# A two-branch kernel on one core: every instruction recorded and issued in the order of a list schedule

## The chip, the cores and the metric

The kernel runs on one core of a Trainium2 chip. The metric is the device time of one execution in microseconds (us), the median of the runs shown. Engines are named as the profile names them: PE (matmul), PEld (its weight loads), DVE (vector), ACT (scalar), POOL, SP. SP and ACT issue transfers from their own instruction streams, and POOL issues some too.

## The reference

Two independent branches are computed on 2048 tokens by 640 channels and concatenated.

Branch A, per channel: a 4-tap shift of `k`, a product with `v`, a causal convolution of length 2048 with the kernel `ssm_k` (by way of a transform), a skip term, a product with `q`:

```
k_shift = sum_t k_pad[:, t:t+S] * shift_k[:, 3-t];   kv = k_shift * v
y = irfft(rfft(kv) * rfft(ssm_k))[:S] + kv * ssm_D;   out_A = q * y
```

Branch B: attention with 32 heads of 20 channels. The 2048 tokens are cut into 4 segments of 512. In each segment there is causal softmax attention, and a memory of the earlier segments:

```
p = softmax(q k^T * scale + mask);  a_dot = p v
a_mem = (phi(q) M) / (phi(q) z + 1e-6)          # phi(t) = t + 1 if t > 0 else exp(t)
o = g * a_mem + (1 - g) * a_dot;   M += phi(k)^T v;  z += sum phi(k)
out_B = concat(o) @ wo
```

## The kernel before, in words

Branch A runs in 5 blocks `dp` of 128 channels. A block loads `sk`, `kr` (transposed by the transfer), `vt` and `qd`; PE does the shift (`pks`, L202) and a forward transform of the kernel and of the product (`pf`, L218), which ACT copies out into `F` (L221); DVE does the butterflies (L229 to L238), the pointwise products (`S`, L251 to L256) and the butterflies back (L261 to L272); PE transforms back (`py`, L283), DVE multiplies by `qd` (`outa`, L284) and POOL stores it (L285).

Branch B runs in 8 units `u`: segment `u // 2`, half `u % 2` of the heads. A unit's projection has four pieces of 128 tokens: 15 matmuls (`kqv`, L312), three copies by ACT (L314), and two transposing transfers on SP that make `KT` (L317) and `QT` (L318). The step `bound` follows: DVE takes a maximum over `KT` (`kam`, L328), PE multiplies (`pb`, L340), ACT copies the result (`bT`, L342) and SP moves it into rows of `QT` by four transfers (L345). POOL spreads `KT` into `KZ` (L377). Then come four groups `g` of four heads: PE makes scores in the banks `stp` (L395), ACT takes their exponential into `ET` (L399, 12 instructions a group, 384 in all), DVE masks (L402), PE multiplies with the values into the one bank `po` (L412, L415), DVE takes a reciprocal (`rr`, L418), multiplies by it (`o2`, L425, or L422 in the first segment) and adds the two parts (L426). After the second half of a segment SP transposes the result (`oT`, L432), PE projects it (`pfo`, L441), ACT copies it out (`outb`, L442) and POOL stores it (L443).

PSUM has eight banks in four pools: three for `stp`, two for A, two for `kqv`, `pb`, `pm` and `pfo`, one for `po`.

The order is set in two steps. The program at L496 to L519 merges lists of pieces by hand-given costs, and the framework's own scheduler then orders the single instructions of the pieces on each engine. Each engine works through its stream in order, an instruction at a time; SP's and POOL's transfers do too, and a transfer that waits holds those behind it.

Of the kernel before, what the change touches and what calls it, by code (L numbers as in the profile page):

```python
# [24 lines left out]
KPAD = 16  # L25
# [34 lines left out]

class K3:
    def __init__(self, ctx, tc, A_q, A_k, A_v, A_shift_k, A_ssm_k, A_ssm_D, B_x, B_wq, B_wk, B_wv, B_wo, B_beta, out):
        self.tc = tc
        nc = self.nc = tc.nc
# [6 lines left out]
        self.a_io2 = E(tc.tile_pool(name="a_io2", bufs=1))  # L71
        self.a_work = E(tc.tile_pool(name="a_work", bufs=1))
        self.a_tmp = E(tc.tile_pool(name="a_tmp", bufs=1))
        self.tmp4 = E(tc.tile_pool(name="tmp4", bufs=1))
        self.b_seg = E(tc.tile_pool(name="b_seg", bufs=1))
        self.b_g = E(tc.tile_pool(name="b_g", bufs=2))
        self.b_small = E(tc.tile_pool(name="b_small", bufs=1))
        self.ps_st = E(tc.tile_pool(name="ps_st", bufs=NST, space=PSUM))
        self.ps_a = E(tc.tile_pool(name="ps_a", bufs=NA, space=PSUM))
        self.ps_b = E(tc.tile_pool(name="ps_b", bufs=NB, space=PSUM))  # L80
        self.ps_o = E(tc.tile_pool(name="ps_o", bufs=NO, space=PSUM))
# [6 lines left out]
        def const(name, arr, dt, eng=nc.gpsimd):  # L88
            t = c.tile(list(arr.shape), dt, name=name)
            eng.dma_start(out=t[:], in_=nc.inline_tensor(arr, name="c_" + name).ap())  # L90
            return t
# [6 lines left out]
        def wload(engs, half):  # L98
# [5 lines left out]
            "Wf": lambda: nc.scalar.dma_start(out=self.Wf[:], in_=nc.inline_tensor(Wf_np, name="c_wf").ap()),  # L104
            "Wi": lambda: nc.sync.dma_start(out=self.Wi[:], in_=nc.inline_tensor(Wi_np, name="c_wi").ap()),
# [50 lines left out]
    def bank(self, pool, name):  # L156
        return pool.tile([128, 512], f32, name=name, tag="bank")

    def a_chunks(self, dp):
# [5 lines left out]
        io, wk = self.a_io2, self.a_work  # L165

        def load_sk():
            sk = io.tile([128, S], bf16, name="sk", tag="kT", bufs=2)
            nc.sync.dma_start(out=sk[:], in_=self.ssm_k[dsl, :])
            skp = io.tile([128, 4, 4, 128], bf16, name="skp", tag="kT", bufs=2)  # L170
            nc.vector.tensor_copy(out=skp[:], in_=sk[:].rearrange("d (b p c) -> d c b p", b=4, c=4))
            Drow = st["Drow"] = io.tile([1, 128], bf16, name="Drow", tag="Drow")
            nc.gpsimd.dma_start(out=Drow[:], in_=self.ssm_D[None, dsl])
            kT = st["kT"] = io.tile([128, 4, 4, 128], bf16, name="kT", tag="kT", bufs=2)
            nc.sync.dma_start_transpose(out=kT[:].rearrange("p c b d -> p (c b) d"), in_=skp[:].rearrange("d c b p -> d (c b p)"))

        def load_kv():
            vt = st["vt"] = io.tile([128, 4, 4, 128], bf16, name="vt", tag="vt")
            for b in range(4):
                (nc.scalar if dp == 0 else nc.sync).dma_start(out=vt[:, b], in_=self.v[512 * b:512 * b + 512, dsl].rearrange("(p c) d -> p c d", c=4))  # L180
            kr = st["kr"] = io.tile([128, 4, KPAD + 512], bf16, name="kr", tag="kr")
# [3 lines left out]
            skd = st["skd"] = io.tile([128, 4, 128], bf16, name="skd", tag="skd")  # L185
# [3 lines left out]
        def load_q():  # L189
            qd = st["qd"] = io.tile([128, 4, 4, 128], bf16, name="qd", tag="qd")  # L190
# [3 lines left out]
        def kshift(b):  # L194
            def f():
                kr, vt = st["kr"], st["vt"]
                ps = self.bank(self.ps_a, "pks")
# [8 lines left out]
        def fwd(kind, c):  # L206
            def f():
                if c == 0:
                    st["F"] = wk.tile([128, 4, 2, 512], bf16, name="F", tag="F")
                F = st["F"]  # L210
                for i in range(2):
                    pf = self.bank(self.ps_a, "pf")
# [28 lines left out]
        def pointwise(b):  # L241
            def f():
                Xv = st["X"][:].rearrange("p (i q) (j a d) -> p i (q j) a d", i=2, j=2, a=2)
                Kv = st["K"][:].rearrange("p (t q) (j b d) -> p t (q j) b d", t=2, j=2, b=2)
                if b == 0:
                    st["S"] = wk.tile([128, 2, 2, 8, 2, 128], bf16, name="S", tag="S")
                Sh = st["S"]
                for i in range(2):
# [3 lines left out]
                    else:  # L252
                        shp = [128, 2, 8, 128]
                        pr = self.a_tmp.tile(shp, bf16, name="pr", tag="pr")
# [19 lines left out]
        def inverse(c):  # L274
            def f():
                U, qd = st["U"], st["qd"]
                outa = self.a_tmp.tile([128, 4, 128], bf16, name="outa", tag="outa", bufs=2)
                py = self.bank(self.ps_a, "py")
# [14 lines left out]
    def b_proj_chunks(self, u):  # L293
# [5 lines left out]
        def load():  # L299
            xT = self.b_seg.tile([128, 5, L], bf16, name="xT", tag="xT")  # L300
# [3 lines left out]
        def proj(tci):  # L304
            def f():
# [3 lines left out]
                for i in range(3):  # L309
                    kq = self.bank(self.ps_b, "kqv")  # L310
# [4 lines left out]
                if tci == 0:  # L315
                    self.KTs[u] = self.b_seg.tile([128, 4, L], bf16, name="KT", tag="KT")
                nc.sync.dma_start_transpose(out=self.KTs[u][:, :, tok], in_=KQ[:, 0, :, :])  # L317
                nc.sync.dma_start_transpose(out=QT[:, :, tok], in_=KQ[:, 1, :, :])  # L318
                if s < NS - 1:
                    xm = self.b_small.tile([128, 2, 16, DH], bf16, name="xm", tag="xm")  # L320
# [5 lines left out]
        def bound():  # L326
            kam = self.b_small.tile([128, 4], f32, name="kam", tag="kam")
            V.tensor_reduce(out=kam[:], in_=self.KTs[u][:], axis=AX.X, op=ALU.max, apply_absolute_value=True)  # L328
            A = self.b_small.tile([128, 4, 16], bf16, name="A", tag="A")
            V.tensor_tensor(out=A[:], in0=self.sel[:], in1=kam[:, :, None].to_broadcast([128, 4, 16]), op=ALU.mult)  # L330
            if s > 0:
                nc.scalar.activation(out=PqT[:], in_=QT[:], func=ACTF.Exp)  # L332
                tq = self.tmp4.tile([128, 4, L], bf16, name="tq", tag="tq")
                V.tensor_scalar(out=tq[:], in0=QT[:], scalar1=1.0, scalar2=1.0, op0=ALU.add, op1=ALU.max)
                V.tensor_tensor(out=PqT[:], in0=PqT[:], in1=tq[:], op=ALU.min)
            qabs = self.tmp4.tile([128, 4, L], bf16, name="qabs", tag="tq")
            V.tensor_scalar(out=qabs[:].bitcast(i16), in0=QT[:].bitcast(i16), scalar1=0x7fff, scalar2=None, op0=ALU.bitwise_and)
# [114 lines left out]
def merge(*lists):  # L452
# [97 lines left out]
```

## Time and profile before

| | |
|---|---|
| median of 3 runs | 390.89 us (390.85 to 393.99) |
| the profiled execution | 391.97 us, span 390.0 us |
| mean granted PE clock | 0.949 |
| first exponential (L399) starts | 62.60 us |
| first exponential of the last unit starts | 341.61 us |
| last exponential ends | 365.73 us |

The span is the time from the first to the last instruction of the profiled execution; its own time is 1.97 us longer. The profile's busy time counts a matmul from its start to its modelled end, so matmuls that follow each other overlap. For the table by stage the span is cut where the first exponential starts, where the last unit's attention starts and where its last exponential ends.

### The profile page before, as it was taken

Reading aid. Unit: us, or ns where it says so; the run is one execution under the profiler, and the core shown is the slowest. Engines: PE = TensorE matmul, PEld = TensorE weight load, DVE = VectorE, ACT = ScalarE, POOL = GpSimd, SP = SyncE. Lnnn points to the kernel's source line nnn. Section 1 sums busy time; section 2 is a strip of 40 time slices with the busy share of each in tenths; the row PEclk is TensorE's granted clock in tenths of the full one; section 3 lists DMA queues with packets and bytes.
Section 4 is the critical chain, followed back from the end, with each engine's and each line's share of the span. In section 5 each row is a group of like instructions: output and inputs, shape, how many; then the busy total and the mean of one; then the engine's idle time right before and its main releaser. Section 6 shows DMA issues by size and latency. Waiting matters only on the chain.

```text
span 390.0 us, 8955 instructions
## 1 busy us (share of the span) xinstructions
PE 326.1 (84%) x3466; PEld 222.3 (57%) x3466; DVE 302.2 (77%) x539; ACT 279.6 (72%) x633; POOL 80.1 (21%) x127
## 2 busy tenths in 40 slices
PE   0499288999989879899979898899989898986854
PEld 0377255565756657467656665577756565644543
DVE  1536299999679969994979999989998938989940
ACT  0067127989898858987777888977789788997402
POOL 8400140202042101231131102132022003410032
PEclk9999869999999989899998999899999999999588
DMA  7999874842246674703863365416620533230052
GB/s 202 272 330 184 171 118 100 141 106 46 58 86 144 107 112 88 150 22 80 180 87 76 59 131 113 94 39 133 116 46 18 100 72 75 57 95 2 0 99 91
DMA packets 110266, 40.96 MB, mean 105 GB/s; under 512 B 102624, under 2 KB 107264, under 8 KB 109968
## 3 DMA queue, kind: packets, MB, share of 16 engines
q1 hardware_dynamic: 100768, 29.50, 39.1%
q0 software_dynamic: 5088, 8.09, 8.0%
q10 hardware_dynamic: 4368, 2.81, 2.5%
q8 instruction: 27, 0.44, 0.5%
q14 instruction: 15, 0.12, 0.1%
HBM read 13.36 MB, written 5.24 MB: 48 GB/s over the span
## 4 chain that ended last, share of the span: by engine, by line
PE 44%; ACT 23%; issue 14%; DMA 9%; DVE 5%; SPq 3%; POOL 2%; POOLq 0%; DVEq 0%; ACTq 0%
ACT ET L399 16%; PE kqv L312 13%; PE stp L395 7%; PE po L412 5%; PE pf L218 5%; PE pfo L441 4%; ACT F L221 3%; PE pks L202 3%; DMA QT<-KQ 3%; DMA xT<-in_B_x_dram 2%; DMA KT<-KQ 2%; PE py L283 2%; PE pb L340 2%; SPq L184 2%; ACT PqT L332 1%
## 5 line engine op out<-in xcount | busy, mean ns | idle before, releaser
L399 ACT ACTIVATE ET<-stp 128x512 bf16<-128x512 f32 (+1 forms) x384 | 172.3, 560 | 15.8 <-PE stp L395 12.6
L395 PE MATMUL stp<-QT,KZ 128*128 128x512 bf16 (+3 forms) x512 | 116.3, 306 | 15.5 <-ACT ET L399 11.4
L312 PE MATMUL kqv<-wqkv,xT 128*128 128x320 bf16 x480 | 82.9, 305 | 1.2 <-DMA xT<-in_B_x_dram 0.9
L395 PEld LDWEIGHTS <-KZ 128*128 128x128 bf16 x512 | 48.2, 99 | 51.0 <-issue 36.0
L377 POOL DMA_DIRECT2D KZ<-KT x64 | 39.8, 624 | 131.2 <-PE stp L395 62.0
L312 PEld LDWEIGHTS <-xT 128*128 128x128 bf16 x480 | 45.7, 99 | 21.3 <-issue 2.9
L221 ACT CAST F<-pf 128x512 bf16<-128x512 f32 x80 | 46.2, 628 | 7.1 <-PE pf L218 5.6
L412 PEld LDWEIGHTS <-ET 128*128 128x128 bf16 x1280 | 42.1, 97 | 14.5 <-DVE o L425 5.3
L402 DVE TENSOR_TENSOR ET<-ET,cmask 128x1024 bf16<-128x1024 bf16 x64 | 41.7, 683 | 9.9 <-ACT ET L399 9.9
L412 PE MATMUL po<-Va,ET 128*128 128x21 bf16 x1280 | 44.3, 174 | 2.8 <-DVE o L425 2.2
L202 PE MATMUL pks<-skd,kr 128*128 128x128 bf16 x320 | 28.0, 241 | 17.4 <-DMA kr<-in_A_k_dram 13.1
L314 ACT CAST KQ<-kqv 128x320 bf16<-128x320 f32 x64 | 27.9, 455 | 19.3 <-PE kqv L312 17.6
L218 PEld LDWEIGHTS <-Wf 128*128 128x128 bf16 x320 | 30.5, 99 | 17.6 <-issue 9.3
L202 PEld LDWEIGHTS <-kr 128*128 128x128 bf16 x320 | 23.6, 109 | 21.3 <-DMA kr<-in_A_k_dram 13.3
L441 PE MATMUL pfo<-wo,oT 128*128 128x320 bf16 x160 | 28.8, 314 | 5.8 <-DMA oT<-o_s 5.3
L285 POOL DMA_DIRECT2D out_dram<-outa x20 | 15.7, 784 | 84.3 <-DVE outa L284 66.8
L442 ACT CAST outb<-pfo 128x320 bf16<-128x320 f32 x32 | 13.3, 451 | 23.4 <-PE pfo L441 20.3
L218 PE MATMUL pf<-kT,Wf 128*128 128x256 bf16 x160 | 26.3, 279 | 4.1 <-ACT F L221 2.7
L418 DVE RECIPROCAL rr<-po 128x16 f32<-128x16 f32 (+1 forms) x64 | 15.5, 243 | 14.4 <-PE po L415 10.9
L283 PE MATMUL py<-S,Wi 128*128 128x256 bf16 x160 | 24.9, 287 | 2.0 <-DVE outa L284 2.0
L218 PE MATMUL pf<-vt,Wf 128*128 128x256 bf16 x160 | 24.5, 279 | 2.2 <-ACT F L221 1.5
L441 PEld LDWEIGHTS <-oT 128*128 128x128 bf16 x160 | 15.6, 101 | 13.6 <-DMA oT<-o_s 6.1
(77 smaller groups left out, 418.0 us busy)
## 6 DMA issues: line engine op xcount, KB each, us to landing
KZ<-KT POOLq DMA_DIRECT2D x64, 42.0 KB, 2.3
sk<-in_A_ssm_k_dram SPq DMA_DIRECT2D x5, 512.0 KB
qd<-in_A_q_dram SPq DMA_DIRECT2D x20, 128.0 KB
out_dram<-outa POOLq DMA_DIRECT2D x20, 128.0 KB, 3.2
out_dram<-outb POOLq DMA_DIRECT2D x16, 160.0 KB, 2.2
vt<-in_A_v_dram SPq DMA_DIRECT2D x16, 128.0 KB
Wf<-c_wf ACTq DMA_DIRECT2D x1, 1024.0 KB
Wi<-c_wi SPq DMA_DIRECT2D x1, 1024.0 KB
```

What stands on the lines that cost most here:

```text
L202: nc.tensor.matmul(ps[:, 128 * c:128 * c + 128], lhsT=kr[:, cc, p0:p0 + 128], rhs=st["skd"][:, t, :], start=(t == 0), stop=(t == 3))
L218: nc.tensor.matmul(o, lhsT=Wf[:, h, c, 256 * i + 128 * j:256 * i + 128 * j + 128], rhs=rhs, start=(h == 0), stop=(h == 1 and not last))
L221: nc.scalar.copy(out=F[:, c, i, :], in_=pf[:])
L283: nc.tensor.matmul(pyv[:, :, h, :], lhsT=Wi[:, k, c, 128 * h:128 * h + 128], rhs=U[:, 4 * i + c, 256 * j:256 * j + 256], start=(k == 0), s ...
L312: nc.tensor.matmul(kq[:, 0:320], lhsT=xT[:, cc, tok], rhs=self.wqkv[:, cc, half, i, :], start=(cc == 0), stop=(cc == 4))
L314: nc.scalar.copy(out=dst, in_=kq[:, 0:320].rearrange("p (h d) -> p h d", d=DH))
L377: nc.gpsimd.dma_start(out=self.KZ[gg][rows, :, hl, :], in_=self.KTs[u][rows, 2 * gg:2 * gg + 2, :])
L395: nc.tensor.matmul(sts[j][:, c0:c0 + n], lhsT=KZ[:, g % 2, hl, 128 * kc:128 * kc + 128], rhs=QT[:, g, 128 * kc:L], start=True, stop=True)
L399: nc.scalar.activation(out=ET[:, 2 * hp + j, e0:e0 + width], in_=sts[j][:, 0:width], func=ACTF.Exp, scale=SCALE)
L402: V.tensor_tensor(out=blk, in0=blk, in1=self.cmask[:, None, None, :].to_broadcast([128, 4, 2, 128]), op=ALU.mult)
L412: nc.tensor.matmul(ops[:, qc % 2, hl, 0:DH + 1], lhsT=ET[:, hl, c0:c0 + 128], rhs=Va[:, kc, 4 * g + hl, 0:DH + 1], start=(kc == 0), stop=( ...
L441: nc.tensor.matmul(pf[:, 0:320], lhsT=oT[:, cc, 128 * tci:128 * tci + 128], rhs=self.wo[:, cc, 320 * i:320 * i + 320], start=(cc == 0), st ...
```

## The change: what it does

No instruction is added or taken away: each engine has as many of each operation after as before (3466 matmuls, 539 on DVE, 633 on ACT, 109 transfers on POOL, 189 on SP, 9 on ACT). The order of all of them is new.

While the kernel's functions run, a recorder stands in place of the engines. It keeps each call, joins the matmuls that follow each other in a bank into one unit, and finds by the regions read and written which units depend on which. Each unit gets a price in ns (on ACT for example its elements per partition over 1.152 plus 33), and a list schedule is made: at every moment an engine that is free takes the ready unit of the highest priority. Priorities come from the length of the way to the end, from a table `BIAS` by stage, and from a pass over the program backwards; six passes are made and the shortest is kept. Transfers of inputs are held back until a time that a pass gives. The schedule also gives out the PSUM banks: a unit that opens a bank is taken only when one of its kind is free. The instructions are then issued in that order, and the framework adds the waits but no order of its own.

Besides, all SBUF tiles are now fixed tiles that are used in turn (`ring`) instead of tiles from pools, the butterfly's temporary `T` lies in the odd planes of its own result instead of in a shared tile, and the score matmuls of a pair of heads are issued bank by bank.

```diff
+    def add(self, eng, method, args, kw):
...
+        if method == "matmul" and bank.last is not None and bank.last.eng == "PE":
+            op = bank.last
...
+    def price(self, op, method, out, ins):
...
+        elif op.eng == "ACT":
+            op.dur, op.lat = n / 1.152 + 33, 210.0
...
+    def forward(self, prio, held):
...
+            for e in free:
+                pe, av = pending[e], avail[e]
+                while pe and pe[0][0] <= t:
+                    i = heapq.heappop(pe)[1]
+                    heapq.heappush(av, (prio[i], i))
+                if free[e] > t:
+                    continue
...
+                    if o.new and (not any(x[0] <= t for x in empty[o.bank.kind]) or (o.bank.row and o.bank.seq != row[o.bank.row])):
+                        put_back.append((p, i))
+                        continue
+                    pick = o
+                    break
...
+                if o.dma is not None:
+                    dma_free = max(dma_free, max(t + 1150, end - 50)) + o.dma
+                    fin = dma_free + 450
+                    near = fin
+                else:
+                    fin, near = end + o.lat, end + (0 if e != "PE" else o.lat)
...
+    def emit(self):
+        for o in self.order:
+            for eng, method, args, kw in o.calls:
...
-                T = self.tmp4.tile([128, 2, 2, 512], bf16, name="T", tag="tq")
-                V.tensor_tensor(out=T[:], in0=F[:, 0:2], in1=F[:, 2:4], op=ALU.add)
+                T = X[:, 1:8:2, :].rearrange("p (c i) r -> p c i r", c=2)
+                V.tensor_tensor(out=T, in0=F[:, 0:2], in1=F[:, 2:4], op=ALU.add)
...
-                        for (kc, c0) in spec:
-                            n = L - 128 * kc
-                            for j in range(2):
-                                hl = 2 * hp + j
+                        for j in range(2):
+                            hl = 2 * hp + j
+                            for (kc, c0) in spec:
+                                n = L - 128 * kc
...
+BANKS = {"st": 3, "a": 2, "b": 2, "o": 1}
+BIAS = {
+    ('A', 0, 0): 5055, ('A', 0, 1): 3361, ('A', 0, 10): 288761, ('A', 0, 11): 15357, ('A', 0, 12): 174774, ('A', 0, 13): 17992, ('A', 0, 14): -17162,
...
-    seq += merge(b_main, a_main)
-    for ch, _ in seq:
-        ch()
+    rec.finish()
+    rec.plan(BIAS, HOLD, PASSES, SLACK)
+    with tc.manual_schedule():
+        rec.emit()
```

Three places show how the order moved. In the changed kernel every instruction has the line of the call in `emit`, L435; its tiles carry the names of the rings. The first place is SP's queue at the start, round the last `KT` transfer of unit 0 (the fourth from `KQ`) and the four transfers of `bT`. Before:

```order
L318 DMA_TRANSPOSE QT_114<-KQ_110 128x4x128
L184 DMA_TRANSPOSE kr<-in_A_k_dram 128x512
L192 DMA qd<-in_A_q_dram 128x4x128 x2
L317 DMA_TRANSPOSE KT<-KQ_109 128x4x128
L318 DMA_TRANSPOSE QT_114<-KQ_109 128x4x128
L192 DMA qd<-in_A_q_dram 128x4x128 x2
L169 DMA sk<-in_A_ssm_k_dram 128x2048
L317 DMA_TRANSPOSE KT<-KQ_110 128x4x128
L318 DMA_TRANSPOSE QT_114<-KQ_110 128x4x128
L180 DMA vt<-in_A_v_dram 128x4x128 x4
L175 DMA_TRANSPOSE kT<-skp 128x16x128
L345 DMA QT_114<-bT 1x4x512 x4
```

Now:

```order
L435 DMA_TRANSPOSE KT_114<-KQ_80 128x4x128
L435 DMA_TRANSPOSE QT_85<-KQ_80 128x4x128
L435 DMA wqkv<-in_B_wq_dram 128x5x320
L435 DMA_TRANSPOSE KT_114<-KQ_81 128x4x128
L435 DMA_TRANSPOSE kr_105<-in_A_k_dram 128x512
L435 DMA_TRANSPOSE QT_85<-KQ_81 128x4x128
L435 DMA_TRANSPOSE kr_105<-in_A_k_dram 128x512 x2
L435 DMA vt_104<-in_A_v_dram 128x4x128
L435 DMA_TRANSPOSE kr_105<-in_A_k_dram 128x512
L435 DMA vt_104<-in_A_v_dram 128x4x128
L435 DMA wqkv<-in_B_wv_dram 128x5x320
L435 DMA vt_104<-in_A_v_dram 128x4x128
```

The second block's `kr` loads, the first block's `qd` loads, one weight load, `Wi` and `wo` stood ahead of the last `KT` transfer and stand behind it now; three of the four `bT` transfers follow the last row shown.

The second place is DVE in the last unit, where the `po` bank is read (`rr`, then the product by `rr`). Before:

```order
L418 RECIPROCAL rr<-po 128x16
L267 TENSOR_TENSOR S<-S 128x2048
L425 TENSOR_TENSOR o_5879<-po,rr 128x320
L269 TENSOR_TENSOR S<-S 128x2x512
L426 TENSOR_TENSOR o_s<-o_5879 128x2x80
```

Now:

```order
L435 RECIPROCAL rr_124<-o_68 128x16
L435 TENSOR_TENSOR o_129<-o_68,rr_124 128x320
L435 TENSOR_TENSOR o_s_120<-o_129 128x2x80
L435 TENSOR_TENSOR S_109<-S_109 128x2048
L435 TENSOR_TENSOR ET_122<-ET_122,cmask 128x4x2x128
```

Of the 64 pairs of a reciprocal and its product, 8 stood next to each other before and 60 do now. Instructions that directly follow the one whose result they read went from 58 to 126 of 539 on DVE.

The third place is ACT where unit 6 begins, between its `bT` copy and its first exponential. Before:

```order
L342 CAST bT<-pb 16x512
L399 ACTIVATE ET<-stp 128x512 x3
L399 ACTIVATE ET<-stp 128x256 x2
L221 CAST F<-pf 128x512
L399 ACTIVATE ET<-stp 128x512 x4
L399 ACTIVATE ET<-stp 128x256 x2
L221 CAST F<-pf 128x512
```

Now:

```order
L435 CAST bT_119<-b_66 16x512
L435 CAST F_102<-a_64 128x512
L435 CAST KQ_80<-b_67 128x16x20
L435 CAST KQ_80<-b_66 128x16x20
L435 CAST Va_84<-b_67 128x16x20
L435 CAST KQ_81<-b_66 128x16x20
L435 CAST KQ_81<-b_67 128x16x20
L435 CAST F_102<-a_65 128x512
L435 CAST Va_84<-b_66 128x16x20
L435 ACTIVATE ET_121<-st_61 128x512
```

Exponentials of unit 5 followed the copy before (11 of them); none is left now, and eight copies stand in between. At the other six beginnings of a unit there were 23, 16, 1, 12, 8 and 18 exponentials left before and there are 26, 15, 11, 4, 14 and 11 now (units 1 to 5, and 7).

## Rows read from the trace of the kernel before

**Rows 1.** The page's first section: busy us (share of the span) xinstructions.

```profile
PE 326.1 (84%) x3466; PEld 222.3 (57%) x3466; DVE 302.2 (77%) x539; ACT 279.6 (72%) x633; POOL 80.1 (21%) x127
```

**Rows 2.** Busy time by stage: length, each engine, clock, transfer share, GB/s.

```profile
0.00:40.00 40.00, 24.47 (x190) 18.38 (x191) 15.85 (x28) 15.42 (x35) 13.64 (x21) 1.00 1.02 244
40.00:62.60 22.60, 14.16 (x126) 10.04 (x126) 15.54 (x20) 3.99 (x10) 5.52 (x9) 0.77 0.73 137
62.60:341.60 279.00, 254.12 (x2798) 173.55 (x2797) 239.62 (x436) 235.85 (x534) 54.62 (x88) 0.98 0.45 91
341.60:365.70 24.10, 18.38 (x209) 9.98 (x207) 22.14 (x37) 21.00 (x49) 1.17 (x2) 0.89 0.15 38
365.70:390.00 24.30, 14.93 (x146) 10.39 (x146) 9.01 (x21) 3.34 (x9) 5.19 (x8) 0.78 0.36 76
```

**Rows 3.** The chain of waits at the start: start, length, what.

```profile
43.61 3.56 DMA QT<-KQ
47.37 2.28 DVE kam L328
50.43 1.88 PE pb L340 x4
```

**Rows 4.** SP's queue in order of time: start, length, what it issues.

```profile
25.61 0.60 SPq L107 DMA_DIRECT2D wo<-in_B_wo_dram  x1
26.31 4.11 SPq L184 DMA_TRANSPOSE kr<-in_A_k_dram  x2
31.79 1.25 SPq L184 DMA_TRANSPOSE kr<-in_A_k_dram  x1
34.41 1.25 SPq L184 DMA_TRANSPOSE kr<-in_A_k_dram  x1
35.71 1.34 SPq L192 DMA_DIRECT2D qd<-in_A_q_dram  x2
39.76 1.25 SPq L192 DMA_DIRECT2D qd<-in_A_q_dram  x2
41.79 1.72 SPq L317 DMA_TRANSPOSE KT<-KQ  x1
52.95 3.04 SPq L345 DMA_DIRECT2D QT<-bT  x4
```

**Rows 5.** ACT in order of time at the start; in brackets the idle time before.

```profile
52.34 0.57 ACT L342 CAST bT<-pb 16x512 bf16<-16x512 f32 x1 [11.86 <-PE pb L340]
62.60 1.57 ACT L399 ACTIVATE ET<-stp 128x512 bf16<-128x512 f32 x3 [2.12 <-PE stp L395]
```

**Rows 6.** DVE's waits from 62.6 to 341.6 us: us in total, times, longest.

```profile
DVE ET L402 <- ACT ET L399: 9.9, 8, 5.3
DVE rr L418 <- PE po L415: 8.0, 13, 1.5
DVE kam L328 <- DMA KT<-KQ: 3.7, 2, 2.9
```

**Rows 7.** DVE in order of time in the last unit.

```profile
367.87 0.48 DVE L425 TENSOR_TENSOR o<-po,rr 128x320 bf16<-128x320 f32 x1
368.26 0.68 DVE L272 TENSOR_TENSOR S<-S 128x1024 bf16<-128x1024 bf16 x1
...
373.58 0.49 DVE L425 TENSOR_TENSOR o<-po,rr 128x320 bf16<-128x320 f32 x1
374.11 0.24 DVE L426 TENSOR_TENSOR o_s<-o 128x160 bf16<-128x160 bf16 x1
```

**Rows 8.** The last unit in order of time: ACT, PE and SP.

```profile
341.61 10.53 ACT L399 ACTIVATE ET<-stp 128x512 bf16<-128x512 f32 x24
360.10 4.31 ACT L399 ACTIVATE ET<-stp 128x512 bf16<-128x512 f32 x9 [1.89 <-PE po L415]
365.94 0.49 PE L412 MATMUL po<-Va,ET 128*128 128x21 bf16 x12 [0.97 <-DVE o L425]
373.01 6.44 SPq L432 DMA_TRANSPOSE oT<-o_s  x4
```

More of the change, by code (lines that the diff above doesn't have):

```diff
@@ L1 @@
+import heapq
 from contextlib import ExitStack
@@ L58, in small_consts, with __init__, __getattr__, call @@
     return sel.astype(BF16_NP), maskbd.astype(BF16_NP), epsrow, cmask.astype(BF16_NP)
+QUEUES = {"sync": "SP", "scalar": "ACT", "vector": "DVE", "tensor": "PE", "gpsimd": "POOL"}
+class Proxy:
+    def __init__(self, rec, name):
+        self.rec, self.name = rec, name
+    def __getattr__(self, method):
+        def call(*args, **kw):
+            self.rec.add(self.name, method, args, kw)
+        return call
+class ProxyNC:
+    def __init__(self, rec):
+        for n in QUEUES:
+            setattr(self, n, Proxy(rec, n))
@@ L70, in __init__ @@
         self.consts = E(tc.tile_pool(name="consts", bufs=1))
[L71 to L81, printed above, removed]
+        self.rings = {}
+        self.real = tc.nc
+        psum = E(tc.tile_pool(name="psum", bufs=1, space=PSUM))
+        for kind, n in BANKS.items():
+            self.rec.add_banks(kind, [psum.tile([128, 512], f32, name=f"{kind}{i}") for i in range(n)])
         Wf_np, Wi_np = dft_tables()
@@ L154, in beta_setup, with bank, ring @@
                             in1=self.epsrow[:, None, :].to_broadcast([128, 4, 4]), op=ALU.mult)
-    def bank(self, pool, name):
-        return pool.tile([128, 512], f32, name=name, tag="bank")
+    def bank(self, kind):
+        return self.rec.bank(kind)
+    def ring(self, name, shape, dt=bf16, n=1):
+        r = self.rings.get(name)
+        if r is None:
+            r = self.rings[name] = [[self.consts.tile(list(shape), dt, name=f"{name}{i}") for i in range(n)], 0]
+        r[1] += 1
+        return r[0][(r[1] - 1) % n]
     def a_chunks(self, dp):
@@ L416, in f @@
                     nb = 1 if s == 0 else 2
-                    rr = self.b_small.tile([128, nb, 8], f32, name="rr", tag="rr", bufs=2)
-                    V.reciprocal(out=rr[:], in_=pov[:, 0:nb, :, DH])
+                    rr = self.ring("rr", [128, 2, 8], f32, n=2)[:, 0:nb]
+                    V.reciprocal(out=rr, in_=pov[:, 0:nb, :, DH])
                     h0 = 16 * half + 4 * g
@@ L497 @@
     K.xTs, K.o_s, K.oT, K.KTs = {}, {}, {}, {}
[L498 to L510 removed]
+    rec = K.rec
+    for name in ("Wf", "w0", "w1", "Wi", "wo"):
+        rec.key = ("load", name)
+        K.deferred[name]()
+    rec.key = ("beta",)
+    K.beta_setup()
+    for dp in range(5):
+        first, second = K.a_chunks(dp)
+        for stage, (f, _) in enumerate(first + second):
+            rec.key = ("A", dp, stage)
+            f()
+    last = []
     for u in range(8):
+        for stage, (f, _) in enumerate(K.b_proj_chunks(u)):
+            rec.key = ("P", u, stage)
+            f()
         pre, at, nt = K.b_attn_chunks(u)
[L513 to L519 removed]
+        for stage, (f, _) in enumerate(pre + at + nt):
+            rec.key = ("T", u, stage)
+            f()
+    rec.finish()
+    rec.plan(BIAS, HOLD, PASSES, SLACK)
+    with tc.manual_schedule():
+        rec.emit()
 _INS = ['A_q', 'A_k', 'A_v', 'A_shift_k', 'A_ssm_k', 'A_ssm_D', 'B_x', 'B_wq', 'B_wk', 'B_wv', 'B_wo', 'B_beta']
```

443 lines of the change are left out of this document (361 added, 82 removed), and 42 rows, old and new, of tables (BIAS, HOLD).

## The prediction

> **What bounds the kernel now.** I read the page's busy times first, then cut the span into stages, then read in each stage what the engines wait for. No engine is full over the span: PE shows 84%, DVE 77%, ACT 72% [rows 1]. The stages are unlike each other [rows 2]. In the first 62.6 us there is no attention: ACT works 19.4 us of them and DVE 31.4. From 0 to 40 us the transfer engines are full (share 1.02, 244 GB/s); from 40 to 62.6 us they no longer are (0.73), and PE, DVE and ACT are all short of work. From 62.6 to 341.6 us, the long middle, DVE is busy 239.6 of 279.0 us and idle 39.4; ACT is idle 43, PE 25. The last unit's attention takes 24.1 us, and 24.3 us follow its last exponential.
>
> What ends the start late is a chain [rows 3]: the last transfer of unit 0's `QT` lands at 47.2 us, DVE takes its maximum until 49.65, PE multiplies until 52.3, ACT copies at 52.3 after 11.9 us of idleness [rows 5], SP moves `bT` from 52.95 to 56.0 [rows 4], and the first exponential starts at 62.6 [rows 5]. The head of that chain is SP's queue: the last `KT` transfer issues at 41.79 us, behind loads that nobody needs yet [rows 4].
>
> In the middle DVE's idle time lies in many places: 9.9 us for `ET` from ACT, 8.0 for `po` from PE, 3.7 for `KT` [rows 6]; these are the three longest. No single wait sets the pace; three engines work in streams whose order makes them miss each other.
>
> **The change, part by part.** The instructions are the same in number and kind, so no busy time goes; what can go is idle time, and what can come is idle time elsewhere.
>
> *The start.* Ahead of the last `KT` transfer SP's order drops one `wo` load (0.60 us of issue), four `kr` loads (4.11 + 1.25 + 1.25) and four `qd` loads (1.34 + 1.25), together 9.8 us [rows 4]; `Wi` and one weight load go too, under 1 us each by the nearest load, `wo`. So the last `KT` issues at about 31 us in place of 41.8. Against it stand two new waits: SP's transpose of the convolution kernel now stands ahead of the first `kr` loads and waits there for a copy by DVE, and `xT` is issued second, so that all large loads run at once. The bytes allow it: `Wi`, `wo`, `qd` and the second block's transposed kernel are 1.05 + 0.82 + 0.52 + 0.52 = 2.9 MB that no longer come ahead of `bT`, at 244 GB/s [rows 2] 12 us. Behind the last `KT` the chain is the same, 20.8 us from its issue to the first exponential (62.6 - 41.8), except that the fourth `bT` transfer now stands behind the next unit's first `KT`, which waits for the spreading by POOL. I take 11 us off: first exponential at 51.6. Bounds: nothing off (62.6) if the loads that now run together delay `xT` and the weights, and 17 off (46) if most of the 6.6 us between the last `bT` issue (56.0) and the first exponential go too. What is moved past the dropped loads comes later: the second block's `kr` and `qd` have the whole of unit 0's attention (48 exponentials, 21 us at 0.44 each, [rows 8]) to land.
>
> *The middle.* DVE is the engine to count: its instructions do not overlap as PE's do, and its 39.4 us of idleness are fewer than ACT's 43. A list order gives DVE and ACT branch A's work wherever attention has nothing ready, and the waits in [rows 6] are of that kind; but the buffers of attention stay as they were: three banks for scores, one `po` bank, one `KT`. I let 27 of the 39.4 us go: the waits for `KT` at a unit's start and others behind transfers, half of the wait for `ET`, most of that for `po`; 12 stay.
>
> A cost comes with it. On DVE 126 instructions instead of 58 now directly follow the one whose result they read. In [rows 7] the product by `rr` is followed after 0.39 us by an instruction that does not need it (367.87 to 368.26) and after 0.53 us by one that does (373.58 to 374.11): 0.14 us more. For 68 pairs that is 9.5 us, 8 of them in the middle. [...]
>
> In return the one `po` bank is held for a shorter time. Before, 56 of 64 pairs had another instruction between reciprocal and product, and PE then waits for the product ([rows 8], 0.97 us of idleness for PE at 365.94) and ACT behind PE (1.89 us at 360.10). That gain is in the 27 us and in the last unit.
>
> So the middle is 239.6 + 8 + 12 = 260, 19 less. Bounds: 248 with no idle time left, 288 with all 39.4 kept and the 8.0 added (rounded).
>
> *The last unit and the end.* Undisturbed, 24 exponentials took 10.53 us [rows 8], so 48 take 21.1 in place of 24.1; I take 22, 2 off. Behind the last exponential there are the mask, the last products, four `oT` transfers (6.4 us, [rows 8]), eight copies and stores: the same chain in both orders, with the last butterflies now earlier against it. I take 1 us off 24.3; bounds 0 and 3.
>
> *At nothing*: the butterfly's `T` in the planes of its result (same instructions, same elements; it frees a tile that three other steps shared), fixed tiles instead of pools, the scores bank by bank. The covers are the same streams; if a fixed tile were taken in turn too soon, the wait would be one of the middle's.
>
> **Sum.** 390.0 - 11 - 19 - 3 = 357 us of span; the profiled execution is 1.97 us longer than its span, so 359, and it lies 1.1 above the median of the runs shown. Forecast: **358 us**, with its own range 342 to 374 (the start between 46 and 60, the middle between 250 and 272).
>
> **Rivals.**
> - *The middle gives nothing.* PE is shown busy 254.1 of 279.0 us, 91% [rows 2]. If PE's stream is the bound, idle time on DVE is only shifted, and the dependent pairs come on top: the middle is 279 + 4 (half of the 8), the start still gives 11, the end 1: 390 - 11 + 4 - 1 + 1 = 383. For it: PE's share. Against it: weight loads, one to a matmul, take 173.6 us there, 62%, and both other engines have the same idle time. [...]
> - *The start gives nothing.* With the transfer engines full until 40 us [rows 2], the loads that are put together only share them; first exponential at 62.6, the rest as forecast: 358 + 11 = 369. For it: share 1.02. Against it: 2.9 MB fewer ahead. 0.05.
> - *Slower: the beginning of a unit is bare.* In unit 0 the time from the `bT` copy to the first exponential is 10.3 us (52.34 to 62.60, [rows 5]). Where exponentials of the unit before are left, they cover it. In the new order none is left at unit 6 and 4 at unit 4. There eight copies stand between, some 4 us at ACT's mean (279.6 us over 633 instructions, 0.44 each, [rows 1]). If that happens at all seven beginnings, 6 us each are bare, 42 us; with the middle's idle time of before kept only in part (20 of 39.4) it is 239.6 + 8 + 20 + 42 = 310, and the time 390 - 11 + 31 - 3 + 1 = 408. It decides from the point where the beginnings cost more than the 33 us forecast as gain, 4.7 us each. Against it: at five of the seven, 11 or more exponentials are left, 4.8 us and more at 0.44 each [rows 8]. 0.08.
> - *The order does not hold on the chip.* The schedule prices the exponentials of a group at 403 ns on average (427 elements over 1.152 plus 33), and they take 439 [rows 8]: 384 of them come 14 us later than planned, so the other engines stand in wrong places and what is won is lost again, 391. Against it: a wait on a late instruction moves all three streams alike. 0.05.
>
> **Chances.** Forecast 0.69. Less than 1%, about 4 us, cannot be told from no change here. Faster by more than that: forecast, and the rivals at 383 and 369, 0.87; within it 0.05; slower 0.08. The range 340 to 384 takes in the forecast's own and the first rival, and leaves out the last two and the thin ends.
>
> **What would show it.** Right: the first exponential near 52 us with the last `KT` issue near 31; from there to the last unit's first exponential about 260 us with DVE over 93% busy; no exponential waiting on `po`. Products by `rr` should follow their reciprocal at once, and DVE's busy time should rise. Wrong: PE busy in the middle without gaps while DVE idles (first rival); ACT gaps of 5 us with "PE stp" as releaser where a unit begins (third); SP idle or waiting in the first 30 us (second).

## The result, and the profile after

The changed kernel takes 357.3 us (median of 4 runs, 355.4 to 361.1) beside 391.8 of the kernel before: ratio 0.910, 95% interval 0.902 to 0.918. Measured once more with the later experiments it took 360.9 us (357.7 to 362.3), ratio 0.921 (0.916 to 0.925). Forecast: 358. Ratios and intervals leave out executions that took over 1.5% longer than the fastest of their kernel; medians do not. The profiled execution took 355.7 us with a span of 353.7.

The page's first section, columns as in [rows 1]: DVE's share is now PE's, 86%, and ACT has risen to 79%.

```profile
PE 302.4 (86%) x3462; PEld 217.8 (62%) x3466; DVE 305.7 (86%) x539; ACT 278.0 (79%) x633; POOL 80.5 (23%) x127
```

The stages, cut at the same events as [rows 2]: first exponential (53.4), first and last exponential of the last unit (308.9 and 332.7).

```profile
0.00:40.00 40.00, 21.26 (x182) 15.45 (x183) 14.00 (x26) 14.97 (x32) 14.27 (x22) 1.00 0.86 192
40.00:53.40 13.40, 10.31 (x110) 7.54 (x110) 13.23 (x21) 5.67 (x13) 5.20 (x9) 1.00 0.65 139
53.40:308.90 255.50, 238.16 (x2803) 173.53 (x2805) 245.82 (x436) 231.92 (x530) 51.84 (x83) 0.98 0.57 112
308.90:332.70 23.80, 19.00 (x256) 11.73 (x254) 23.35 (x43) 22.04 (x53) 4.02 (x7) 1.00 0.13 38
332.70:353.70 21.00, 13.71 (x116) 9.57 (x116) 9.35 (x17) 3.44 (x9) 5.21 (x8) 0.75 0.35 89
```

The start is 9.2 us shorter, the middle 23.5, the last unit 0.3, the end 3.3: together the 36.3 us between the spans. In the middle DVE is busy 245.8 of 255.5 us, 96%; its idle time fell from 39.4 to 9.7 us. The waits that were 9.9, 8.0 and 3.7 us [rows 6] are 0.4, 0.4 and 0.6 (DVE's waits from 53.4 to 308.9 us: total, times, longest):

```profile
DVE o_s L435 <- DMA oT<-o_s: 1.5, 1, 1.5
DVE Xh L435 <- ACT F L435: 1.5, 1, 1.5
...
DVE kam L435 <- DMA KT<-KQ: 0.6, 1, 0.6
DVE rr L435 <- PE o L435: 0.4, 1, 0.4
DVE ET L435 <- ACT ET L435: 0.4, 1, 0.4
```

SP's queue at the start answers to [rows 4]: nothing of `wo` or `qd` stands ahead of unit 0's last key transpose, which issues at 35.18 us (41.79 before).

```profile
1.21 7.91 SPq L435 DMA_TRANSPOSE xT<-in_B_x_dram  x1
...
27.85 0.47 SPq L435 DMA_DIRECT2D kT<-in_A_ssm_k_dram  x1
30.91 2.25 SPq L435 DMA_TRANSPOSE KT<-KQ  x1
33.24 1.22 SPq L435 DMA_TRANSPOSE QT<-KQ  x1
34.52 0.57 SPq L435 DMA_DIRECT2D wqkv<-in_B_wq_dram  x1
35.18 1.19 SPq L435 DMA_TRANSPOSE KT<-KQ  x1
```

ACT at the start answers to [rows 5]: the copy that the last key transpose takes ends at 34.7, `bT`'s copy begins at 44.99 where it was 52.34, the first exponential at 53.43.

```profile
34.29 0.43 ACT L435 CAST KQ<-b 128x320 bf16<-128x320 f32 x1 [1.15 <-PE b L435]
...
44.99 0.57 ACT L435 CAST bT<-b 16x512 bf16<-16x512 f32 x1 [3.07 <-PE b L435]
...
53.43 0.60 ACT L435 ACTIVATE ET<-st 128x512 bf16<-128x512 f32 x1
```

DVE in order of time shows both kinds of neighbour as in [rows 7]. The product `o`, 0.49 us long, is followed after 0.41 us by an instruction that does not read it (306.81 to 307.22), so that the two overlap, and after 0.52 by one that does (312.92 to 313.44). The reciprocal's product follows after 0.28 us.

```profile
306.53 0.25 DVE L435 RECIPROCAL rr<-o 128x16 f32<-128x16 f32 x1
306.81 0.49 DVE L435 TENSOR_TENSOR o<-o,rr 128x320 bf16<-128x320 f32 x1
307.22 0.68 DVE L435 TENSOR_TENSOR Kh<-F 128x1024 bf16<-128x1024 bf16 x1
...
312.92 0.49 DVE L435 TENSOR_TENSOR o<-o,rr 128x320 bf16<-128x320 f32 x1
313.44 0.24 DVE L435 TENSOR_TENSOR o_s<-o 128x160 bf16<-128x160 bf16 x1
```

At the end the last `oT` transposes begin 3.9 us after the last exponential (332.7), where in [rows 8] it was 7.3 (373.01 against 365.7): these are the 3.3 us.

```profile
336.63 7.67 SPq L435 DMA_TRANSPOSE oT<-o_s  x4
```

### The profile page after: what moved, and what is told of

Same layout as the page of the kernel before. It is cut to its first block, busy times and chain, and to the rows that moved or that the text cites. A ratio compares the mean times of both kernels' runs of the same rounds, so it can differ in the third digit from the quotient of the medians.

```text
span 353.7 us, 9016 instructions
## 1 busy us (share of the span) xinstructions
PE 302.4 (86%) x3462; PEld 217.8 (62%) x3466; DVE 305.7 (86%) x539; ACT 278.0 (79%) x633; POOL 80.5 (23%) x127
## 4 chain that ended last, share of the span: by engine, by line
PE 33%; DVE 28%; issue 14%; DMA 8%; ACT 6%; SPq 6%; POOL 3%; POOLq 0%; ACTq 0%; DVEq 0%
PE b L435 13%; PE a L435 9%; PE st L435 7%; DVE S L435 7%; SPq L435 6%; PE o L435 4%; DVE ET L435 4%; DMA KT<-KQ 3%; DVE Xh L435 3%; ACT ET L435 3%; DVE kam L435 3%; DMA kr<-in_A_k_dram 2%; POOL out_dram L435 2%; DMA oT<-o_s 1%; DVE o L435 1%
## 5 line engine op out<-in xcount | busy, mean ns | idle before, releaser
L435 ACT ACTIVATE ET<-st 128x512 bf16<-128x512 f32 (+1 forms) x384 | 185.2, 575 | 11.6 <-PE st L435 10.5
L435 PE MATMUL st<-QT,KZ 128*128 128x384 bf16 (+2 forms) x508 | 105.1, 301 | 6.3 <-ACT ET L435 3.9
L435 PE MATMUL b<-wqkv,xT 128*128 128x320 bf16 x480 | 79.3, 303 | 18.8 <-DMA xT<-in_B_x_dram 16.0
L435 PEld LDWEIGHTS <-xT 128*128 128x128 bf16 x480 | 45.8, 99 | 37.6 <-DMA xT<-in_B_x_dram 16.0
L435 POOL DMA_DIRECT2D KZ<-KT x64 | 40.0, 629 | 123.0 <-PE st L435 91.1
L435 PEld LDWEIGHTS <-KZ 128*128 128x128 bf16 x512 | 45.6, 98 | 28.0 <-issue 12.2
L435 PEld LDWEIGHTS <-ET 128*128 128x128 bf16 x1280 | 41.8, 96 | 24.1 <-DVE ET L435 11.5
L435 PE MATMUL o<-Va,ET 128*128 128x21 bf16 x1280 | 44.2, 173 | 12.0 <-DVE ET L435 5.9
L435 ACT CAST F<-a 128x512 bf16<-128x512 f32 x80 | 48.4, 624 | 5.5 <-PE a L435 5.0
L435 ACT CAST KQ<-b 128x320 bf16<-128x320 f32 x64 | 30.0, 472 | 19.4 <-PE b L435 17.4
L435 DVE TENSOR_TENSOR ET<-ET,cmask 128x1024 bf16<-128x1024 bf16 x64 | 43.0, 682 | 0.4 <-ACT ET L435 0.4
L435 PEld LDWEIGHTS <-Wf 128*128 128x128 bf16 x320 | 30.3, 99 | 15.8 <-issue 8.8
L435 DVE TENSOR_TENSOR S<-S 128x2048 bf16<-128x2048 bf16 (+1 forms) x40 | 37.2, 950 | 0.2
L435 POOL DMA_DIRECT2D out_dram<-outa x20 | 15.4, 769 | 71.5 <-DVE outa L435 52.7
L435 PE MATMUL b<-wo,oT 128*128 128x320 bf16 x160 | 28.0, 314 | 0.6 <-DMA oT<-o_s 0.6
L435 PE MATMUL a<-kT,Wf 128*128 128x256 bf16 x160 | 24.3, 274 | 2.9 <-DVE outa L435 1.9
L435 ACT CAST outb<-b 128x320 bf16<-128x320 f32 x32 | 14.9, 480 | 14.1 <-PE b L435 14.1
L435 DVE TENSOR_TENSOR o<-o,rr 128x320 bf16<-128x320 f32 x48 | 23.6, 491 | 1.6
L435 PE MATMUL a<-vt,Wf 128*128 128x256 bf16 x160 | 23.3, 280 | 1.4 <-ACT F L435 0.7
L435 PE MATMUL a<-S,Wi 128*128 128x256 bf16 x160 | 22.2, 286 | 1.5 <-DVE S L435 1.5
L435 DVE TENSOR_TENSOR S<-Xh,Kh 128x4096 bf16<-128x4096 bf16 x10 | 22.8, 2284 | 0.1
L435 PE MATMUL a<-skd,kr 128*128 128x128 bf16 x320 | 22.0, 224 | 0.4 <-DMA kr<-in_A_k_dram 0.2
```

Of the source, the lines that this page charges most:

```text
L435: f(*[fix(a) for a in args], **{k: fix(v) for k, v in kw.items()})
```

## The experiments

Theory: the order of single instructions took away DVE's idle time, SP's order brought the start forward, and the middle is now bound by DVE. Rivals: the fixed tiles did it; the tables did it; the start is made up anyway; PE and ACT bind as much as DVE.

Medians in us, ratio to the kernel before with its 95% interval:

| run | median | ratio |
|---|---|---|
| e1_tiles_only | 397.2 | 1.012 (1.004 to 1.020) |
| e2_merged_as_is | 675.4 | 1.722 (1.712 to 1.733) |
| e3_no_tables | 363.3 | 0.927 (0.922 to 0.933) |
| e4_start_undone | 374.9 | 0.944 (0.936 to 0.951) |
| r1_after_again | 360.9 | 0.921 (0.916 to 0.925) |
| e5_pairs_apart | 357.0 | 0.909 (0.904 to 0.915) |
| e7_off_dve | 366.9 | 0.934 (0.928 to 0.939) |
| e8_wf_late | 354.6 | 0.906 (0.902 to 0.910) |
| e6_after_one_mask | 350.0 | 0.892 (0.888 to 0.895) |
| e6_before_one_mask | 395.3 | 1.007 (1.004 to 1.011) |
| e9_apart_wf_late | 352.2 | 0.898 (0.894 to 0.902) |
| e10_apart_wf_later | 353.0 | 0.898 (0.894 to 0.902) |

The time from the first to the last exponential, read for each kernel from the rows of `ET`, is what the order does once the start is over. How far it is steady shows in two executions of the changed kernel, 278.9 and 277.7 us; before it was 302.7 (62.6 to 365.3). The row of the tile `ET` (minimum, median, maximum ns; first and last start) in the second of them:

```profile
L435 ACT ACTIVATE ET<-st x384: 356/597/1047, 61.0 to 338.7; 128x512 bf16<-128x512 f32 x126, 128x256 bf16<-128x256 f32 x66
```

**Buffers without the order.** The recorded instructions come in the order of the old merge, and the framework's scheduler orders them; the plan of the PSUM banks goes with the order.

```diff
-    rec.plan(BIAS, HOLD, PASSES, SLACK)
-    with tc.manual_schedule():
-        rec.emit()
...
+    for o in rec.ops:
+        for eng, method, args, kw in o.calls:
+            getattr(getattr(rec.real, eng), method)(*args, **kw)
```

> The changed kernel's buffers and pieces (ring tiles that are allocated once, the butterfly's T in planes of Xh, scores emitted bank by bank, banks handed out in turn) with the old piece-by-piece merge and the framework's own scheduler, so that only the order and the bank plan are undone. Theory (the order is the gain): about 391 us, 383 to 399, with the first exponential near 62 us and DVE idle 30 to 45 us in the middle. Rival (the fixed tiles give the freedom, whoever orders the work): under 372 us, with DVE idle below 20 us in the middle.

397.2 us, and 306.6 us from the first to the last exponential. DVE is idle 44.9 us of it and waits as before, most of all for `po`; its three longest waits there:

```profile
DVE rr L959 <- PE o L959: 17.5, 27, 2.6
DVE kam L959 <- DMA KT<-KQ: 9.1, 5, 2.9
DVE ET L959 <- ACT ET L959: 8.5, 6, 4.3
```

The rival falls: tiles, planes and score order alone gain nothing. The order and the bank plan were taken away together; what each is worth by itself was not tried.

**The merge's order as it stands.** As above, but inside `manual_schedule`.

> The same recorded instructions issued word for word in the order in which the old merge writes them, with no scheduling of single instructions at all. Theory: slower than the kernel before, 400 to 470 us, since every engine's queue then stands behind the first late operand (a piece's exponentials, its mask and its products follow one another with nothing between). Rival (the merge already sets the order, and a scheduler of single instructions adds little): 380 to 400 us.

675.4 us, far beyond the theory's 470. All engines wait in turn, DVE 49% busy and ACT 43%, and the mean granted PE clock is 0.75 where it was 0.95; PE is shown busy for 410.3 us with the same matmuls, 326.1 before [rows 1]:

```profile
PE 410.3 (61%) x3434; PEld 257.2 (38%) x3466; DVE 326.3 (49%) x539; ACT 287.2 (43%) x633; POOL 79.5 (12%) x127
```

So the old scheduler was worth 278 us of its own (675.4 to 397.2), and the new order is 36 to 40 us better than that.

**The tables emptied.**

```diff
-BIAS = { ... }
-HOLD = { ... }
+BIAS = {}
+HOLD = {}
```

> The changed kernel with both tables of numbers emptied: the list schedule goes by the longest chain to the end and its six passes alone. Theory: the list schedule gives part of the gain and the tables the rest; 365 to 385 us, DVE idle in the middle between the 9.7 us of the changed kernel and the 39.4 us of before. Rival A (the planner alone does it): 354 to 362 us. Rival B (without the tables it is no better than the old scheduler): over 388 us.

363.3 us, between the theory's span and rival A's, and 283.4 us from the first to the last exponential. The list schedule alone gives 29 us; the tables add 4.5 to 5.7 us there and 2 to 6 in the run. In the run that is clear of noise beside the first measurement of the changed kernel (intervals 0.922 to 0.933 and 0.902 to 0.918), not beside the second (0.916 to 0.925).

**The start undone.**

```diff
+    early = {("A", 0, 16), ("load", "Wi"), ("load", "wo"), ("A", 1, 0)}
+    ...   # their 10 transfers on SP go ahead of unit 0's last KT transpose
```

> The changed kernel's order, but the key transposes of the second feature block (4 of 1.25 us), the four query loads of the first one and the loads of Wi and wo (6 of 0.6 us) stand on SP's queue ahead of unit 0's last key transpose again. Theory (the start is worth its time one for one): 9 us of issues more ahead of that transpose, its issue near 44 us where it was 35.2, the first exponential near 62 where it was 53.4, and the run 7 to 10 us longer, 363 to 368 us. Rival (the middle has DVE work to put there, so that a late first exponential is made up): under 3 us longer.

374.9 us, about 370 by its ratio: both more than the theory's 363 to 368. The rows of PE's first matmul and of `ET` tell why:

```profile
22.44 6.66 PE L435 MATMUL b<-wqkv,xT 128*128 128x320 bf16 x30 [22.44 <-DMA xT<-in_B_x_dram]
```

```profile
L435 ACT ACTIVATE ET<-st x384: 357/598/1029, 71.4 to 347.5; 128x512 bf16<-128x512 f32 x126, 128x256 bf16<-128x256 f32 x66
```

Here `x` landed at 22.44 us; in the changed kernel's first profile at 16.03, in its second at 23.61, with nothing different ahead of it:

```profile
16.03 5.59 PE L435 MATMUL b<-wqkv,xT 128*128 128x320 bf16 x30 [16.03 <-DMA xT<-in_B_x_dram]
```

```profile
23.61 6.58 PE L435 MATMUL b<-wqkv,xT 128*128 128x320 bf16 x28 [23.61 <-DMA xT<-in_B_x_dram]
```

From there to the first exponential it is 37.4 us in both (53.4 and 61.0), and 49.0 with the ten transfers back. So 11.6 us are the edit's, and the rest is scatter of that landing. Of the 11.6, 2 are made up later (276.1 us to the last exponential). The rival of a start that is made up falls. Before, the stretch was 43.8 us (first such matmul at 18.8 us).

A part of these 11.6 us goes with PE's clock, which no expectation named. The rows of `pb`'s four matmuls before, in the changed kernel and with the ten transfers back, with PE's idle time in brackets:

```profile
50.43 1.88 PE L340 MATMUL pb<-qabs,A 128*16 128x512 bf16 x4 [8.39 <-DVE A L330]
```

```profile
43.92 1.03 PE L435 MATMUL b<-tq,A 128*16 128x512 bf16 x4 [2.62 <-DVE A L435]
```

```profile
60.45 1.88 PE L435 MATMUL b<-tq,A 128*16 128x512 bf16 x4 [13.09 <-DVE A L435]
```

Before, PE had stood for 8.39 us and its granted clock was 0.50 from 48 to 56 us; in the changed kernel it had stood for 2.62 us and the clock is 1.00 from 44 to 52 us. With the transfers back PE stands for 13.09 us and the clock is 0.50 again (60 to 64 us; 0.90 in the mean of the first 71.4 us). The same matmuls in the same order, from `pb` to the first scores, take 10.46 us there (60.45 to 70.91) and 8.99 in the changed kernel (43.92 to 52.91): some 1.5 of the 11.6 us go with the lower clock.

**The changed kernel again.**

> The changed kernel once more, as the common measure for the three that follow on the same chip. Both theories: 355 to 361 us as before; its start differs from execution to execution (the issue of the first x transpose, which takes 7.9 us in the profile of the changed kernel), so that differences below 2 us between these four are not read.

360.9 us, within its span.

**Dependent neighbours set apart.** After the plan:

```diff
...
+    for a, b, c in zip(dve, dve[1:], dve[2:]):
+        i = at[b.idx]
+        if a.calls[0][1] == "reciprocal" and a.idx in b.pred and c.dur < 900 and all(at[p] < i for p in c.pred):
+            q.remove(c)
+            q.insert(i, c)
...
```

> The changed kernel's order, but at 35 of the 64 places where a reciprocal and its product stand side by side on DVE the next other instruction of DVE (under 0.9 us) is put between them, as the old scheduler had it. Theory A (the price of a dependent neighbour counts now that DVE is the bound): DVE's busy time falls by 35 x 0.12 = 4 us, and the run by 2 to 4 us. Theory B (the one PSUM bank of the products is what the order protects): PE's waits for that bank, 3.5 us in the middle, grow by up to 35 x 0.6 = 21 us of which DVE idle takes a part, and the run is 3 to 15 us longer.

357.0 us, 3.9 less, with intervals apart. DVE's busy time falls by 4.1 us (305.8 to 301.7), 0.117 us for each of 35 pairs; the first line is of the kernel above, the second of this one:

```profile
PE 302.8 (84%) x3462; PEld 217.0 (60%) x3466; DVE 305.8 (85%) x539; ACT 277.8 (77%) x633; POOL 81.3 (23%) x127
PE 302.1 (84%) x3462; PEld 217.7 (61%) x3466; DVE 301.7 (84%) x539; ACT 277.3 (77%) x633; POOL 81.3 (23%) x127
```

First to last exponential takes 274.4 us, and with the same edit 273.9 in e9 and 276.5 in e10, beside 277.7 to 278.9 in the two executions of the changed kernel and in e8:

```profile
L435 ACT ACTIVATE ET<-st x384: 356/597/1085, 64.4 to 338.8; 128x512 bf16<-128x512 f32 x126, 128x256 bf16<-128x256 f32 x66
```

Theory A holds. B falls: from 64 to 338 us PE's waits of `po`'s matmuls for the products total 5.3 us (5.5 in the kernel above, same stretch).

**Work moved off DVE.** In blocks 1 to 4, at the same places of the order, ACT makes the copies of `kT` and GpSimd the products for `skd`.

```diff
+    for o in rec.order:
+        if o.eng == "DVE" and o.calls[0][1] == "tensor_copy" and o.key[0] == "A" and o.key[1] > 0:
+            o.calls = [("scalar", "copy", [], dict(out=o.calls[0][3]["out"], in_=o.calls[0][3]["in_"]))]
+        elif o.eng == "DVE" and o.calls[0][3]["out"].tensor.name.startswith("skd") and o.key[1] > 0:
+            o.calls = [("gpsimd",) + o.calls[0][1:]]
```

> The changed kernel's order, but four copies of kT (1.22 us each) are ScalarE's and four products for skd (0.68 us each) GpSimd's where they were VectorE's, at the same places of the order. Theory (DVE is the bound of the middle, 96% busy): 7.6 us less on DVE and 4 to 7 us off the run. Rival 1 (PE and ACT, with 17 and 24 us of idle time in 255, bind as much): under 2 us off. Rival 2 (GpSimd's product takes long and holds up VectorE or the keys' shift): slower by 2 us or more.

366.9 us, 6 longer: the theory falls, and the second rival's number came. DVE's busy time fell by 2.9 us and not 7.6; 3.7 us of the difference are four of DVE's products of two SBUF operands that ran beside GpSimd's and took longer. GpSimd at 99.12 and 134.95 us, then DVE (two such products alone take 1.28):

```profile
99.12 1.05 POOL L435 TENSOR_TENSOR skd<-ident,skc 128x512 bf16<-128x512 bf16 x1
134.95 1.05 POOL L435 TENSOR_TENSOR skd<-ident,skc 128x512 bf16<-128x512 bf16 x1
```

```profile
97.94 2.79 DVE L435 TENSOR_TENSOR Xh<-Xh 128x1024 bf16<-128x1024 bf16 x2
...
135.24 1.92 DVE L435 TENSOR_TENSOR Xh<-Xh 128x1024 bf16<-128x1024 bf16 x2
```

And DVE's idle time between first and last exponential rose from 8.8 to 15.1 us: it now waits for `po` (2.1) and for exponentials (1.8) of an ACT with 5 us more to do. How the 4.7 us of that stretch divide between the two was not tried.

**Wf later.**

```diff
...
+    rec.order.remove(late)
...
+    rec.order.insert(first, late)
```

Here `late` is Wf's load on ACT's queue, and `first` the first copy of a projection, which follows the first load of `v`.

> The changed kernel's order, but the load of Wf (1 MB) is issued on ACT's queue behind the first load of v, ahead of the first copies, where it stood ahead of that load. Theory (the first x transpose lands late, at 16.0 us, because 1 MB of Wf goes ahead of it, and the start counts one for one): x lands 2 to 4 us earlier, the first exponential comes 2 to 4 us earlier and the run is 2 to 4 us shorter. Rival (the transpose's own issue, 7.9 us, sets when it lands): no change beyond 1 us.

354.6 us, 6.3 less than the second measurement of the changed kernel (intervals apart) and 2.7 less than the first (intervals overlap). Its runs lie between 353.0 and 356.5. In its one profile `x` is first used at 17.16 us, where six profiles with the unedited head show 16.03 to 26.88. The theory's direction holds. That the edit takes the late landings away, and does not make all of them earlier, is the likely reading; one profile here and one of e9 (17.25 us) do not show it.

**One mask of two left out, in both kernels.** It leaves the upper triangle of half the diagonal blocks unmasked. So in the kernel before; in the changed kernel the same 32 instructions are dropped from the planned order.

```diff
-for (c0, step) in ((0, 512), (896, 128)):
+for (c0, step) in ((0, 512),):
```

> Leaves out part of the computation: the second of the two causal masks of each group of heads (32 of 64 mask products, 0.68 us each, about 0.6 us of DVE's time apart), at the changed kernel's order. Theory (DVE binds the middle): 19 to 22 us less on DVE, and 12 to 18 us off the run, until PE (22 us idle from the first to the last exponential) and ACT (25 us idle) bind. Rival (PE, ACT and DVE bind one another in turn, as the run with work moved off DVE suggests): under 8 us off.

> Leaves out the same 32 masks in the kernel before. Theory (there the order's waits, not DVE's work, set the time: 39.4 us of DVE idle in the middle): 3 to 10 us off. Rival (DVE's work bound that kernel as much): as many us off as in the changed kernel, 12 or more.

The kernel before gains nothing from 17.1 us less of DVE's work (302.2 to 285.1 busy): 395.3 us, where 3 to 10 less were expected. The changed kernel takes 350.0, 7 to 11 less. Both views by stage, from first to last exponential:

```profile
64.70:375.40 310.70, 277.32 (x3054) 185.94 (x3053) 249.64 (x449) 256.34 (x582) 57.59 (x90) 0.96 0.42 85
```

```profile
61.10:329.80 268.70, 254.31 (x3060) 184.21 (x3058) 252.07 (x445) 251.75 (x582) 56.35 (x89) 0.99 0.54 110
```

The two halves are not alike. In the changed kernel the order is given, and DVE's other 475 instructions follow one another as they did; before, the framework's scheduler made a new order without the masks, and DVE's instructions stand in another one. There DVE's idle time grows to 61.1 us: what was taken away came back as waits. That speaks for waits as the bound of the kernel before, but does not show it for the order that it had; for that there are the 39.4 us of idle time and the gain of 23.5 us with no work left out. In the changed kernel 17.1 us less of work shorten the stretch by 9.0 to 10.2, between theory and rival; then PE, DVE and ACT are busy within 3 us of one another. DVE binds the changed kernel, but PE and ACT (256 and 253 us busy in its 278, DVE 269) are close behind:

```profile
61.00:338.70 277.70, 256.13 (x3056) 183.82 (x3058) 268.91 (x476) 253.36 (x582) 55.87 (x89) 0.99 0.55 106
```

**The two that helped, together, and Wf later still.** e9 joins the edits of e5 and e8; e10 has Wf behind the first copy:

```diff
-    rec.order.insert(first, late)
+    rec.order.insert(first + 1, late)
```

> The two edits that helped together: 35 products set apart from their reciprocal, and Wf's load behind the first load of v. Theory (one works in the middle, the other at the start, so they add): 4 us and 6 us off the 360.9 of the changed kernel's second measurement, 349 to 353 us. Rival (the late start of the unedited order was partly made up in the middle, so they overlap): 353 to 356 us.

> As the one before, but Wf's load stands behind the first copy of a projection on ACT's queue, so that x's transpose has landed before its 1 MB is asked for. Theory (the 1 MB that goes beside x's transpose delays it): x lands 2 to 5 us earlier than with Wf behind the first load of v, and the run is 2 to 4 us shorter still, 346 to 350 us. Rival A (x's transpose is slow for its own sake): no change from the one before. Rival B (Wf is then late for the first transforms): 2 us longer or more.

e9: 352.2 us, in its theory's span, and faster than both kernels (its interval lies wholly below that of the second measurement of the changed kernel). e10: 353.0, no change: rival A by its number. But not by its reason: `x` was first used at 11.75 us, 5.5 earlier than in e9, as the theory has it, and ACT then stood for 4.72 us with a load of `v` ahead of its next copy, until `kr` had landed.

```profile
21.83 0.43 ACT L435 CAST KQ<-b 128x320 bf16<-128x320 f32 x1 [4.72 <-DMA kr<-in_A_k_dram]
```

The first exponential came at 54.9 us, 43.1 after that. One wait took the place of another.

## Why the prediction was right, step by step

- **The middle, 19 off: 23.5.** Of DVE's idle 39.4 us 29.7 went (27 forecast), and its busy time rose by 6.2 (8 forecast). No exponential waits for `po` now (2.8 us before). e1 and e3 show that the order, with its bank plan, did it, e6 that the kernel is now bound mostly by DVE; that waits bound it before rests on their 39.4 us.
- **The dependent neighbours.** At 0.14 us each the price was near: e5 gives 0.117. But 68 pairs were to add 9.5 us, and DVE's busy time rose by 3.5 in all (302.2 to 305.7). About two thirds of the middle's 6.2 is work that moved in: the start lost 4.2 us of DVE's busy time (31.4 to 27.2). So the 8 us were too much, and that the middle's busy time came out near owes to a shift that the prediction did not count. The prediction also says that DVE's instructions do not overlap as PE's do, and the text on the kernel before that each engine takes an instruction at a time. PE's overlap more: ten projection matmuls, 0.30 us each in the median, take 1.52 us there (60.82 us). But [rows 7] show that DVE's overlap too, by some 0.1 us (0.48 us long, the next after 0.39), and it is this overlap that a dependent neighbour loses.
- **The start, 11 off: 9.2 in the profile, 1.6 in the second one** (62.6 to 61.0). The mechanism held, the term was mis-sized. The order's own part is 6.4 us (43.8 to 37.4 from `x`'s landing to the first exponential); undoing ten transfers alone costs 11.6. The rest hangs on when `x` lands, 18.8 us before and 16.0 to 26.9 now. The sentence that failed is "The bytes allow it": they do over the whole start, but not ahead of `x`, whose transpose was put beside all large loads and whose issue took 7.9 to 12.5 us (4.5 before). The last key transpose was at 35.2 and not 31, since the copy that it takes ended only at 34.7. So it came 6.6 us earlier (41.79 to 35.18). The chain behind it was to stay the same at 20.8 us and took 18.2, 2.6 less: PE's granted clock, which the prediction left out, was 0.50 for a part of it before and is 1.00 now, worth some 1.5 us by e4.
- **The last unit, 2 off: 0.3.** I took the 48 exponentials as its bound; DVE was busy 23.35 of 23.8 us there, with branch A's last products between. **The end, 1 off: 3.3**, by the earlier `oT` transposes. The two errors, 1.8 and 2.3 us, nearly cancel.
- **The rivals.** The middle gave its share, so 383 fell (its chance was 0.13, which is 0.87 less 0.69 and 0.05); PE's shown busy time there fell too, from 254.1 to 238.2 us at the same clock of 0.98 and with as many matmuls, so it was no floor. Order not holding on the chip (391) fell with the 23.5 us. Bare beginnings of units (408): no idle time of ACT in the middle that PE's scores end is longer than 1.7 us, where 4.7 each was the point of decision. The start's rival (369) was nearer than its 0.05: with the second profile's start the gain there is all but gone, and the sign named for it was there, since SP stood for 2.6 us ahead of the transpose at 30.91 us.
- **Two bounds** do not come out of their terms: 239.6 + 39.4 + 8 is 287 and not 288, and a start at 60 with a middle of 272 gives 378 and not 374. The result lies far from both.

That the median came out within 1 us owes something to luck: the middle and the end gave 6.8 us more than forecast, the start and the last unit 3.6 less, and the median lies 1.6 us above the profiled execution where I put it 1.1 below.

## What to carry to other kernels

When three engines are each 75 to 90% busy and idle in many short waits, take the busy time of the fullest engine as the floor and ask which idle time an order can close; leaving a known piece of work out tells whether an engine binds, if the order of the rest is kept (9 to 10 of 17 us here; the 0 us before are of a new order). Read a start from the landing of its first operand on, since the landing itself can differ: here by 7.6 us between two executions of the same program, and by nearly 11 among six with the same head. Don't put large loads beside it (`x`'s issue took 7.9 to 12.5 us here with Wf asked for at 2.4 us, 6.4 to 6.7 with it at 5.3 us or later). Look at PE's granted clock behind a long wait (0.50 behind 8.39 us here, 1.00 behind 2.62). Once one engine is full, its own price of neighbours counts (0.117 us a pair in e5), and moving its work to other engines can cost more than it saves (e7: DVE 2.9 us less busy, the run 6 us longer).

## What the runs showed of the hardware

- The issue of `x`'s first transposing transfer (0.66 MB) held SP for 7.9 to 12.5 us in six executions with Wf's 1 MB asked for at 2.4 us, and for 6.4 to 6.7 us in three with Wf at 5.3 us or later.
- Beside a GpSimd product of 1.05 us, DVE products of two SBUF operands took 0.4 to 1.5 us longer (`Kh` below 1.04 us, its mean in the changed kernel 0.68), while one that reads PSUM kept its 0.68 us (e7, GpSimd at 40.40 us, then DVE):

```profile
40.40 1.03 POOL L435 TENSOR_TENSOR skd<-ident,skc 128x512 bf16<-128x512 bf16 x1
```

```profile
40.34 0.68 DVE L435 TENSOR_TENSOR vt<-a,vt 128x512 bf16<-128x512 f32 x1
40.94 1.04 DVE L435 TENSOR_TENSOR Kh<-Kh 128x1024 bf16<-128x1024 bf16 x1
```

  What holds DVE's products up is not shown. Two of the four had started 0.3 and 0.6 us before GpSimd's, by a profile whose times on GpSimd are rough.
